# Attention with normalized queries and keys, then an MLP: a new order for batch 0, four score tiles in some bursts, and 64 by 64 tiles for three batches

## Chip, cores and metric

The kernel runs on one core of a Trainium2 chip, in one launch. The metric is the time of one execution on the device, in microseconds (us). Four executions of the kernel before gave 436.19 to 438.37, with a median of 438.2.

## What is computed

```python
B, H, S, D = 8, 12, 448, 64          # batches, heads, positions, head size
q_n, k_n = rmsnorm(q, g_q), rmsnorm(k, g_k)
attn = softmax(q_n @ k_n.T / 8)      # each batch and head by itself
x = (attn @ v) -> (B * S, H * D)     # heads side by side: 3584 x 768
h = x @ w_in                         # w_in 768 x 2048
g = max(h, 0) + alpha * min(h, 0)    # alpha per column of h, between 0 and 0.3
out = g @ w_out                      # w_out 2048 x 768, out 3584 x 768, float32
```

## The kernel before, in words

**Groups.** The 12 heads of a batch are handled in 3 groups of 4 heads (two pairs in each half of the partitions); groups are numbered through all batches, so batch b has groups 3b, 3b+1 and 3b+2, 24 in all. In a group's score tile (`score`, line 223) keys lie on the 128 partitions: 64 keys of two heads, with 448 queries for each of two columns ("par"). A group has 7 such tiles (j from 0 to 6). Each tile is exponentiated by ScalarE (`soft`, line 241, with a constant in place of the maximum) from PSUM into fp16. There are two PSUM buffers for score tiles.

**Tiles of the array.** Scores contract over 64 rows and so use half of the array's rows per matmul. Line 226 sets how many columns one matmul takes: 64 in batch 0 (4 matmuls to a tile), 32 in all other batches (8 matmuls to a tile). `over_keys` (line 249) sums over keys, with the exponentials as the moving operand: for the softmax's denominators (`den`, weights of ones) and for the values (`attv`). It works on a pair of groups (the first two of a batch, always 32 columns: 56 matmuls) or on the batch's third group by itself (line 251: 64 columns for group 2, 28 matmuls, else 32 columns, 56 matmuls). For a pair, `attv` runs twice, for even columns of the values (half 0) and for odd ones (half 1).

**PSUM.** There are three pools: two buffers of two banks for scores ("sc"), one buffer of two banks for denominators, values and turns ("acc"), and two single banks for the MLP ("mm"). Half 0 of the values goes to "acc" and half 1 to the two "mm" banks. A step may use "acc" in place of an "mm" bank when the plan calls it spare (`bank`, line 313; names hTa and opa in the profile).

**Preparing queries and keys.** For each group: load (SP's queue, `load_qk`), square (POOL), sum of squares (`reduce`, VectorE), `root` (ScalarE: a log and an exponential), scaling to fp16 (`scale`, mostly POOL), and a transposition. The first 6 groups are transposed by PE and copied out of PSUM by VectorE (`turn`, line 186; tiles tps in "mm", tps2 in "acc"). The others are transposed by DMA on SP's queue (`turn_dma`), and `turn` then only multiplies K by the gains on VectorE.

**MLP.** `up` (line 342) is one block of 128 columns of h: 6 matmuls, then ScalarE multiplies by alpha and VectorE takes the maximum into gT. `down` (line 355) is one 128 by 384 block of the output: 16 matmuls, a copy by VectorE, and two stores on SP's queue. For batch 0 the first four `up` blocks are begun before the last third of their input is there (`begin`, line 333) and finished later.

**The order of the work** is written out by the program before anything is issued; no scheduler reorders it. Lines 389 to 425 pack score tiles into numbered bursts of 2 or 3 tiles, and say in which burst the denominators (`dens`) and the values (`avs`) of a pair or a group fall. Lines 435 to 467 attach loads, squares, sums, roots and turns to bursts. Lines 470 to 539 share `up` and `down` steps out over the bursts, by estimated costs. The loop at line 589 then issues burst by burst: up to two score tiles, their exponentials, denominators or values, a third tile (and for pairs the second half of the values behind it), then the MLP steps of the burst. Within an engine, and within a DMA queue, instructions run in that order. Idle stretches of PE early on are filled with matmuls whose output is not used (`spin`). "First full unit" below is the first `up` that was not begun early: 6 matmuls at 46.16 us.

Of the kernel before, what the change touches and what calls it, by code (L numbers as in the profile page):

```python
# [21 lines left out]
def kernel(  # L22
# [17 lines left out]
    J = S // 64  # L40
    HH = H // 2
    G = HH // 2
# [5 lines left out]
    FB = DF // 4  # L48
    TD = min(6, NG)
    EB = 3  # L50
    assert G == 3

    cst = ctx.enter_context(tc.tile_pool(name="cst", bufs=1))
# [132 lines left out]
    def turn(y):  # L186

        if y >= TD:
            t = qkT[y, "k"].rearrange("p j g c -> p (j g c)")
            nc.vector.tensor_scalar(  # L190
                out=t, in0=t, scalar1=gain[:, 0:1], scalar2=None, op0=ALU.mult
            )
            return
        if y < G:
            ps = [psf.tile([128, 512], FP32, name="tps", tag="mm") for _ in "qk"]
        else:
            ps2 = psa.tile([128, 2, 512], FP32, name="tps2", tag="acc")
            ps = [ps2[:, 0], ps2[:, 1]]
        tps = [
            t[:, : S].bitcast(FP16).rearrange("p (j c) -> p j c", j=J) for t in ps  # L200
        ]
        for tp, nm in zip(tps, "qk"):
            for j in range(J):
                nc.tensor.transpose(  # L204
                    tp[:, j, :], qs[y, nm][:, j].rearrange("p h d -> p (h d)"), ident
                )
        for tp, nm in zip(tps, "qk"):
            t = att.tile([128, J, 2, 64], FP16, name=f"{nm}T", tag=f"{nm}T", bufs=4)
            o = t.rearrange("p j g c -> p j (g c)")
            if nm == "q" and y == 0:  # L210
                nc.scalar.copy(out=o, in_=tp)
            elif nm == "q":
                nc.vector.tensor_copy(out=o, in_=tp)
            else:
                nc.vector.tensor_scalar(  # L215
                    out=o, in0=tp, scalar1=gain[:, 0:1], scalar2=None, op0=ALU.mult
                )
            qkT[y, nm] = t
# [4 lines left out]
    def score(y, j):  # L223
        qT, kT = qkT[y, "q"], qkT[y, "k"]
        sc = pss.tile([128, 2, 512], FP32, name="sc", tag="sc")
        m = 64 if y < G else 32
        for c in range(64 // m):
            for par in range(2):
                for g in range(2):
                    nc.tensor.matmul(  # L230
                        out=sc[ds(64 * g + m * c, m), par, :S].rearrange(
                            "p (j c) -> p j c", j=J
                        ),
                        lhsT=kT[ds(64 * par, 64), j, g, ts(c, m)],
                        rhs=qT[ds(64 * par, 64), :, g, :],
                        start=True,
                        stop=True,
                    )
        scs[y, j] = sc

    def soft(y, j):
        if j == 0:
            expT[y] = att.tile([128, J, 2, S], FP16, name="expT", tag="expT", bufs=EB)
        nc.scalar.activation(  # L244
            out=expT[y][:, j], in_=scs[y, j][:, :, :S], func=AF.Exp,
            scale=QK_SCALE, bias=expb[:, 0:1],
        )

    def over_keys(accs, ys, weights):

        m = 64 if ys == (G - 1,) else 32
        if len(ys) == 2:
            heads = [(y, par, 0) for y in ys for par in range(2)]
        else:
            heads = [(ys[0], par, c) for par in range(2) for c in range(64 // m)]
        for j in range(J):
            for h, (y, par, c) in enumerate(heads):
                for g in range(2):
                    nc.tensor.matmul(  # L259
                        out=accs[g][ds(m * h, m), :S],  # L260
                        lhsT=weights(g, y, par, ts(c, m), j),
                        rhs=expT[y][ds(64 * g, 64), j, par, :],
                        start=(j == 0),
                        stop=(j == J - 1),
                    )
# [17 lines left out]
    def attv(ys, half, spare=False, jobs=()):  # L283

        b, i = divmod(ys[0], G)
        v2 = vt[b].rearrange("p h j (d e) -> p h j d e", e=2)

        def weights(g, y, par, c, j):
            h = 2 * (y - G * b) + par
            if len(ys) == 1:  # L290
                return vt[b][ds(64 * g, 64), h, j, c]
            return v2[ds(64 * g, 64), h, j, :, half]

        if half:
            av, accs = None, [psf.tile([128, 512], FP32, name="avb", tag="mm") for _ in range(2)]
        else:
            pool, tag = (pss, "sc") if spare else (psa, "acc")
            av = pool.tile([128, 2, 512], FP32, name="av", tag=tag)
            accs = (av[:, 0], av[:, 1])
        over_keys(accs, ys, weights)  # L300
        for f in jobs:
            f(ys)
        if b not in xT:
            xT[b] = att.tile([128, 2, G, S], FP16, name="xT", tag="xT")
        x, r = xT[b][:, :, i + half, :], rden[ys]
        if half:
            for g in range(2):
                nc.vector.tensor_mul(out=x[:, g], in0=accs[g][:, :S], in1=r[:, g])
        else:
            nc.vector.tensor_mul(out=x, in0=av[:, :, :S], in1=r)  # L310
# [22 lines left out]
    def begin(ft):  # L333

        if ft < 2:
            begun[ft] = bank("hT", False)
        elif ft == 2:
            t = psa.tile([128, 2, 512], FP32, name="hTb", tag="acc")
            begun[2], begun[3] = t[:, 0], t[:, 1]
        up_part(begun[ft], 0, ft, 0, G - 1)  # L340
# [55 lines left out]
    while m < NG * J or steps:  # L396
        n = len(bursts)
        while steps:
            ys, values = steps[0]
            if values:  # L400

                if n in dens and ys != (G - 1,):
                    break
                avs[n] = ys
                av_at.update((y, n) for y in ys)
            else:
                if n in avs or any(last_in.get(y, n) >= n for y in ys):
                    break
                dens[n] = ys
                den_at.update((y, n) for y in ys)  # L410
            steps.pop(0)
        late = len(avs.get(n, ())) == 2 or n in dens and n in avs or any(y >= G for y in dens.get(n, avs.get(n, ())))
        bursts.append([])
        while len(bursts[n]) < (3 if late else 2) and m < NG * J:
            y, j = divmod(m, J)
            if j == 0 and y >= EB and av_at.get(y - EB, n) == n:

                if y - EB not in av_at:
                    break
                split[n] = min(len(bursts[n]), 2)  # L420
            bursts[n].append((y, j))
            first_in.setdefault(y, n)
            if j == J - 1:
                last_in[y] = n
            m += 1
# [10 lines left out]
        y: max(n for n in range(first_in[y]) if y >= TD or n not in dens)  # L436
        for y in range(1, NG)
    }
    turn_at[2] = 5
    turn_at.update((y, den_at[y - 2]) for y in range(TD, NG) if y % G == 1)  # L440
    turns = {n: y for y, n in turn_at.items()}
    jobs = {}
    for y in range(G, NG):

        early = y < G + 2
        if early:
            n = turn_at[y - 1] + (y == G)
        elif y == G + 2:
            n = den_at[G - 1]
        elif y == 2 * G:  # L450
            n = turn_at[y] - 4
        elif y == 2 * G + 1:
            n = den_at[G] - 1
        elif y % G:
            n = den_at[y - 3 if y % G == 1 else y - G]
        else:
            n = av_at[y - 4]
        at(n - (6 if early else 4 if y <= 3 * G else 5), load_qk, y)
        for nm in "qk":
            (after if early else at)(n - 2, square, y, nm)  # L460
            if early:
                after(n, reduce, y, nm)
            else:
                jobs.setdefault(n, []).append((reduce, (y, nm)))
        roots[n + 1] = y
# [123 lines left out]
    for n in range(NB):  # L589
# [5 lines left out]
        first_tiles = tiles[: split.get(n, 2)] if not lead else tiles  # L595
        for t in first_tiles:
            score(*t)
            if lead and t == tiles[0]:
                soft(*t)
                den(dens[n])  # L600
                attv(avs[n], 0, True, (log, invert))
            elif lead and t == tiles[1]:
                begin(1)
                begin(2)
        plain = lead or n not in dens and n not in avs
        wait = plain and not lead and gaps[n] and gaps[n][0][0] is up
# [4 lines left out]
        if n in dens and not lead:  # L611
            den(dens[n])
        if n in avs and not lead:
            attv(avs[n], 0)
        for t in tiles[len(first_tiles) :]:
            score(*t)
            soft(*t)
        if n in avs and len(avs[n]) == 2:
            attv(avs[n], 1)
        late = []  # L620
        if wait:
            late = [(1, soft, t) for t in tiles[1:]]
# [50 lines left out]
                    late = []  # L673
        if not gaps[n] and n in turns:
            turn(turns[n])
        if n == den_at[G - 1] - 1:
            begin(0)
        for _, g, c in late:
            g(*c)
        if n < den_at[G - 1] - 1 and plain and n not in turns:  # L680
# [35 lines left out]
```

## Time and profile before

| what | value |
|---|---|
| median of four executions | 438.2 us |
| the profiled execution | 438.37 us, of which its span is 436.6 us |
| mean granted clock of TensorE | 0.994 |
| PE busy | 416.0 us, 5241 matmuls and as many weight loads |
| ScalarE (ACT) busy | 277.2 us |
| VectorE (DVE) busy | 208.9 us |
| POOL busy | 175.6 us |
| DMA | 53.88 MB, mean 123 GB/s over the span |
| 16 matmuls of `down`, between two others | 2.60 us |
| 6 matmuls of `up`, between two others | 1.14 us |
| one exponential of a score tile (ACT) | 1.00 us, 0.93 in a row |

How to read the profile: PE is TensorE's stream of matmuls, PEld its weight loads beside it. A row of the order of time gives the start, the length, the engine, the line of the kernel, the operation, output and inputs, the tile of the array (64*32: 64 rows by 32 columns), the shape, a count of equal instructions in a row, and in brackets the idle time before it with what ended it. The ends of matmuls are modelled, so lengths of runs are best taken from start to start. "issue" is a wait that ends on nothing the profile shows. In the waits by releaser the numbers are the total in us, how often, and the longest.

### The profile page before, as it was taken

Reading aid. Unit: us, or ns where it says so; the run is one execution under the profiler, and the core shown is the slowest. Engines: PE = TensorE matmul, PEld = TensorE weight load, DVE = VectorE, ACT = ScalarE, POOL = GpSimd, SP = SyncE. Lnnn points to the kernel's source line nnn. Section 1 sums busy time; section 2 is a strip of 40 time slices with the busy share of each in tenths; the row PEclk is TensorE's granted clock in tenths of the full one; section 3 lists DMA queues with packets and bytes.
Section 4 is the critical chain, followed back from the end, with each engine's and each line's share of the span. In section 5 each row is a group of like instructions: output and inputs, shape, how many; then the busy total and the mean of one; then the engine's idle time right before and its main releaser. Section 6 shows DMA issues by size and latency. Waiting matters only on the chain.

```text
span 436.6 us, 12032 instructions
## 1 busy us (share of the span) xinstructions
PE 416.0 (95%) x5241; PEld 215.2 (49%) x5241; DVE 208.9 (48%) x303; ACT 277.2 (63%) x385; POOL 175.6 (40%) x133
## 2 busy tenths in 40 slices
PE   7779999799999999999999999999999999999996
PEld 3334445354555445544555445444555445555563
DVE  3756664444574356535554356535553353233421
ACT  4897888368977576768847576758837577132300
POOL 5799878436273625283073625174043000000000
PEclk9999999989999999999999999999999999999999
DMA  8999999988449831997069841984064300211033
GB/s 191 238 231 199 207 236 187 198 178 179 95 82 185 194 96 25 168 186 179 21 113 177 183 101 26 174 163 110 20 101 102 77 1 21 57 37 36 20 73 73
DMA packets 70229, 53.88 MB, mean 123 GB/s; under 512 B 37392, under 2 KB 70176, under 8 KB 70176
## 3 DMA queue, kind: packets, MB, share of 16 engines
q1 hardware_dynamic: 55456, 40.19, 42.9%
q0 software_dynamic: 13984, 11.81, 18.4%
q10 hardware_dynamic: 736, 1.11, 1.0%
q8 instruction: 41, 0.67, 0.6%
q14 instruction: 12, 0.10, 0.1%
HBM read 45.62 MB, written 11.01 MB: 130 GB/s over the span
## 4 chain that ended last, share of the span: by engine, by line
PE 87%; ACT 6%; DVE 3%; issue 2%; DMA 1%; SPq 0%; ACTq 0%
PE op L359 29%; PE hT L325 20%; PE hTa L325 10%; PE sc L230 8%; PE opa L359 6%; PE dn L259 5%; PE av L259 5%; ACT expT L244 3%; PE avb L259 3%; DMA nat<-in_k_dram 1%; ACT ah L352 1%; DVE ss L152 1%; DVE gT L353 1%; PE tps L204 1%; DVE kT L215 0%
## 5 line engine op out<-in xcount | busy, mean ns | idle before, releaser
L244 ACT ACTIVATE expT<-sc,expb 128x896 f16<-128x896 f32 x168 | 160.4, 1003 | 41.4 <-PE sc L230 40.6
L359 PE MATMUL op<-w_out_sb,gT 128*128 128x384 f16 x752 | 131.2, 330 | 0.0
L169 POOL TENSOR_TENSOR qs<-nat,rr 128x896 f16<-128x896 f32 x44 | 76.7, 1761 | 111.9 <-ACT rr L164 82.4
L359 PEld LDWEIGHTS <-gT 128*128 128x128 f16 x896 | 85.0, 98 | 67.3 <-issue 14.7
L325 PEld LDWEIGHTS <-w_in_sb 128*128 128x128 f16 x768 | 73.2, 98 | 73.6 <-issue 9.2
L325 PE MATMUL hT<-xT,w_in_sb 128*128 128x448 f16 x516 | 108.1, 353 | 0.9 <-DVE gT L353 0.9
L146 POOL TENSOR_TENSOR sq<-nat 128x896 f32<-128x896 f32 x44 | 73.2, 1679 | 49.0 <-DMA nat<-in_q_dram 23.7
L352 ACT ACTIVATE ah<-hT,cols 128x448 f16<-128x448 f32 x86 | 54.3, 633 | 47.3 <-PE hT L325 47.3
L353 DVE TENSOR_TENSOR gT<-hT,ah 128x448 f16<-128x448 f32 x86 | 53.6, 624 | 56.5 <-ACT ah L352 56.4
L369 DVE COPY osb<-op 128x384 f32<-128x384 f32 x47 | 26.2, 557 | 80.1 <-PE op L359 77.5
L230 PE MATMUL sc<-qT,kT 64*32 64x448 f16 (+1 forms) x1260 | 53.3, 355 | 7.1 <-ACT expT L244 4.3
L152 DVE TENSOR_REDUCE ss<-sq 128x14 f32<-128x896 f32 x48 | 49.9, 1077 | 7.0 <-ACT sq L144 6.2
L325 PE MATMUL hTa<-xT,w_in_sb 128*128 128x448 f16 x240 | 51.9, 353 | 0.0
L352 ACT ACTIVATE ah<-hTa,cols 128x448 f16<-128x448 f32 x40 | 25.4, 634 | 31.4 <-PE hTa L325 31.4
L353 DVE TENSOR_TENSOR gT<-hTa,ah 128x448 f16<-128x448 f32 x40 | 25.0, 624 | 28.5 <-ACT ah L352 28.5
L230 PEld LDWEIGHTS <-kT 64*32 64x32 f16 (+1 forms) x1260 | 15.2, 90 | 37.9 <-issue 32.5
L310 DVE TENSOR_TENSOR xT<-av,rden 128x896 f16<-128x896 f32 x16 | 17.5, 1092 | 21.2 <-PE av L259 19.3
L259 PE MATMUL dn<-expT,ones 64*32 64x448 f16 (+1 forms) x868 | 24.5, 350 | 2.9 <-issue 2.1
L259 PEld LDWEIGHTS <-vt 64*32 64x32 f16 (+1 forms) x1316 | 19.5, 93 | 14.2 <-issue 2.9
L359 PE MATMUL opa<-w_out_sb,gT 128*128 128x384 f16 x144 | 24.9, 327 | 0.0
L259 PE MATMUL av<-expT,vt 64*32 64x448 f16 (+1 forms) x868 | 24.1, 349 | 0.7 <-ACT rden L276 0.7
L259 PEld LDWEIGHTS <-ones 64*32 64x32 f16 (+1 forms) x868 | 13.0, 93 | 11.7 <-issue 4.3
(43 smaller groups left out, 163.2 us busy)
## 6 DMA issues: line engine op xcount, KB each, us to landing
out_dram<-osb SPq DMA_DIRECT2D x110, 96.0 KB, 2.3
nat<-in_q_dram SPq DMA_DIRECT2D x46, 224.0 KB, 4.9
nat<-in_k_dram SPq DMA_DIRECT2D x46, 224.0 KB, 5.6
vt<-in_v_dram POOLq DMA_DIRECT2D x16, 336.0 KB, 6.8
w_in_sb<-in_moe_w_in_dram POOLq DMA_DIRECT2D x12, 256.0 KB, 7.5
w_out_sb<-in_moe_w_out_dram POOLq DMA_DIRECT2D x4, 768.0 KB, 15.4
nat<-in_q_dram ACTq DMA_DIRECT2D x2, 224.0 KB, 4.7
nat<-in_k_dram ACTq DMA_DIRECT2D x2, 224.0 KB, 6.0
```

The source lines that it names most:

```text
L146: nc.gpsimd.tensor_mul(out=sqf, in0=src, in1=src)
L152: nc.vector.tensor_reduce(out=ss_t[y][:, "qk".index(nm)].rearrange("p h j -> p (h j)").unsqueeze(2), in_=sqs[y, nm], axis=AXIS_X, op=ALU.add,)
L169: eng.tensor_mul(out=t.rearrange("p j h d -> p h j d"), in0=nat[y, nm], in1=rr_t[y][:, "qk".index(nm)].unsqueeze(3).broadcast_to((128, 2, ...
L230: nc.tensor.matmul(out=sc[ds(64 * g + m * c, m), par, :S].rearrange("p (j c) -> p j c", j=J), lhsT=kT[ds(64 * par, 64), j, g, ts(c, m)], r ...
L244: nc.scalar.activation(out=expT[y][:, j], in_=scs[y, j][:, :, :S], func=AF.Exp, scale=QK_SCALE, bias=expb[:, 0:1],)
L259: nc.tensor.matmul(out=accs[g][ds(m * h, m), :S], lhsT=weights(g, y, par, ts(c, m), j), rhs=expT[y][ds(64 * g, 64), j, par, :], start=(j = ...
L310: nc.vector.tensor_mul(out=x, in0=av[:, :, :S], in1=r)
L325: nc.tensor.matmul(out=hT[:, :S], lhsT=w_in_sb[:, g * G + i, ts(ft, 128)], rhs=xT[b][:, g, i, :], start=(i == 0 and g == 0), stop=(i == G ...
L352: nc.scalar.activation(out=ah, in_=hT[:, :S], func=AF.Copy, scale=alpha_sb[:, ft : ft + 1])
L353: nc.vector.tensor_max(out=gT[:, ft, ds((b & 1) * S, S)], in0=hT[:, :S], in1=ah)
L359: nc.tensor.matmul(out=op[:, :OH], lhsT=gT[:, ft, ts(t, 128)], rhs=w_out_sb[:, ft, ds(oh * OH, OH)], start=(ft == 0), stop=(ft == NF - 1),)
L369: nc.vector.tensor_copy(out=o, in_=op[:, :OH])
```

## The change

- A constant `EARLY = 3 * G` makes groups 0 to 8 (batches 0 to 2) use 64 columns per matmul for scores, and groups 2, 5 and 8 for denominators and values by themselves.
- A burst with the values of a pair from batch 1 on may hold four score tiles. The fourth comes after the second half of the values, and it may be the first tile of a group whose exponentials take over the buffer that these values free. Three bursts fewer are needed (69 in place of 72). Turns and preparations attached to bursts shift with that: the first group of a batch is scaled and transposed by DMA in the burst of the pair's denominators, no longer in that of its values.
- In batch 0, odd columns of the first pair's values come first, then even ones, then the third score tile and behind it the turn of group 3, which now uses the "mm" banks. The first two early `up` blocks come in the burst after that, ahead of its exponentials.
- Due times: preparations of group 6 are attached one burst earlier, so that its sums fall between `up` steps. In the order of the queues, group 6's squares come before group 5's scaling on POOL, and group 6's DMA transposes before group 8's loads on SP.

In the program's order, 280 matmuls and 280 weight loads fewer are issued. The core of the diff:

```diff
+    EARLY = 3 * G
...
-        if y < G:
+        if y <= G:
             ps = [psf.tile([128, 512], FP32, name="tps", tag="mm") for _ in "qk"]
...
-        m = 64 if y < G else 32
+        m = 64 if y < EARLY else 32
...
-        m = 64 if ys == (G - 1,) else 32
+        m = 64 if len(ys) == 1 and ys[0] < EARLY else 32
...
-        late = len(avs.get(n, ())) == 2 or n in dens and n in avs or any(y >= G for y in dens.get(n, avs.get(n, ())))
+        both = len(avs.get(n, ())) == 2
+        late = both or n in dens and n in avs or any(
+            y >= G for y in dens.get(n, avs.get(n, ()))
+        )
+        limit = 2 + late + (both and avs[n][0] >= G)
         bursts.append([])
-        while len(bursts[n]) < (3 if late else 2) and m < NG * J:
+        while len(bursts[n]) < limit and m < NG * J:
             y, j = divmod(m, J)
             if j == 0 and y >= EB and av_at.get(y - EB, n) == n:
 
-                if y - EB not in av_at:
+                if y - EB not in av_at or both and len(bursts[n]) < 3:
                     break
...
-    turn_at[2] = 5
+    turn_at[2], turn_at[G] = 5, av_at[0]
...
-            n = turn_at[y - 1] + (y == G)
+            n = turn_at[y - 1] + 1
...
-        elif y == 2 * G + 1:
-            n = den_at[G] - 1
+        elif y % G == 1:
+            n = den_at[y - 4] - 1
         elif y % G:
-            n = den_at[y - 3 if y % G == 1 else y - G]
+            n = den_at[y - G]
...
             score(*t)
-            if lead and t == tiles[0]:
+            if n == den_at[G - 1] - 1 and t == tiles[-1]:
+                begin(0)
+                begin(1)
+            elif lead and t == tiles[0]:
                 soft(*t)
                 den(dens[n])
                 attv(avs[n], 0, True, (log, invert))
             elif lead and t == tiles[1]:
-                begin(1)
                 begin(2)
...
-            attv(avs[n], 0)
-        for t in tiles[len(first_tiles) :]:
+
+            for half in (1, 0) if avs[n] == (0, 1) else (0,):
+                attv(avs[n], half)
+        for t in tiles[len(first_tiles) : 3]:
             score(*t)
             soft(*t)
-        if n in avs and len(avs[n]) == 2:
+        if n in avs and len(avs[n]) == 2 and avs[n] != (0, 1):
             attv(avs[n], 1)
+        for t in tiles[max(len(first_tiles), 3) :]:
+            score(*t)
+            soft(*t)
...
-        if n == den_at[G - 1] - 1:
-            begin(0)
```

## Prediction

> **What bounds the kernel now.** I read the chain of waits first, then PE's order of time, then PE's own waits, then the clock stage by stage. The chain says where a saving counts:
>
> ```profile
> PE 87%; ACT 6%; DVE 3%; issue 2%; DMA 1%; SPq 0%; ACTq 0%
> ```
>
> TensorE (PE) is 87% of the chain. From the first MLP unit at 46.16 us to PE's last matmul at 432.3 us it is hardly ever idle, so there a microsecond counts only if it is one of PE. Before 46 us the chain runs through ScalarE's exponentials and the first turns. A second item is small but concentrated: "issue", 2%. PE's waits by releaser, without any time of day:
>
> ```profile
> PE sc L230 <- ACT expT L244: 4.3, 10, 0.7
> PE dn L259 <- issue: 2.1, 1, 2.1
> PE avb L259 <- issue: 0.9, 1, 0.9
> PE sc L230 <- issue: 0.8, 1, 0.8
> PE dn L259 <- DVE osb L369: 0.6, 1, 0.6
> ```
>
> Three waits release on nothing the profile shows. PE's order of time places two of them (start, duration, tile, count, idle before):
>
> ```profile
> 76.44 0.57 PE L259 MATMUL avb<-expT,vt 64*32 64x448 f16 x12
> 77.88 1.32 PE L259 MATMUL avb<-expT,vt 64*32 64x448 f16 x44 [0.88 <-issue]
> 79.13 2.77 PE L359 MATMUL opa<-w_out_sb,gT 128*128 128x384 f16 x16
> 81.84 0.57 PE L230 MATMUL sc<-qT,kT 64*32 64x448 f16 x16
> 82.56 1.50 PE L259 MATMUL dn<-expT,ones 64*32 64x448 f16 x52
> 86.13 0.37 PE L259 MATMUL dn<-expT,ones 64*32 64x448 f16 x4 [2.08 <-issue]
> 86.15 0.55 PE L230 MATMUL sc<-qT,kT 64*32 64x448 f16 x8
> 86.62 4.45 PE L359 MATMUL op<-w_out_sb,gT 128*128 128x384 f16 x16
> ```
>
> Both stops fall in the middle of a run of equal matmuls, so no operand is missing. Between them lie 44+16+16+52 = 128 matmuls, each with its weight load: 256 instructions. The third stop (280.96 us) lies 5376 = 21x256 instructions further, PE's separate waits counted. And a queue of its own carries instructions:
>
> ```profile
> q8 instruction: 41, 0.67, 0.6%
> ```
>
> 0.67 MB in 41 packets is 16 KB each. I read: PE's program arrives in blocks of 256 instructions, a block is asked for when the one before it starts, and PE stops when that took longer than a block lasts (71.15 to 77.88 us: 6.7 us; 77.88 to 86.13: 8.3 us; 275.50 to 282.11: 6.6 us). The second stop costs more than itself (PE's busy time, then the other engines', clock, DMA share):
>
> ```profile
> 83.51:86.92 3.41, 1.33 (x34) 0.45 (x19) 0.98 (x1) 0.83 (x2) 3.10 (x4) 1.00 1.27 183
> 86.92:90.33 3.41, 3.41 (x13) 1.67 (x11) 0.45 (x1) 2.61 (x3) 0.08 (x1) 0.50 1.05 185
> ```
>
> After 3.4 us with PE 39% busy the clock is 0.50 for the next 3.4 us, and op needs 4.39 us start to start instead of 2.71.
>
> Price of the stops, start to start against the same run undisturbed: avb 2.69-1.43, dn 3.59-1.32, sc and op at half clock 0.18+1.68, sc at 281 1.44-0.30: **6.5 us**.
>
> **The change part by part.** The profiled execution took 438.37 us (span 436.6), 0.2 above the median; sums are against it.
>
> *64 by 64 tiles for groups 3 to 8.* A score tile is 4 matmuls instead of 8, a single group's den or values 28 instead of 56: 6x7x4 + 4x28 = 280 matmuls and 280 weight loads fewer. Streaming gains nothing: 28 matmuls of 64x64 take 1.35 us (38.29 to 39.64), 56 of 64x32 take 1.32. What it costs is switches. Pairs of groups keep 64x32, so scores and pairs now differ. The Trainium skill ("TensorEngine Tiling (Array Packing)", Key Properties) says that changing the tiling mode drains the array, which speaks against this. The rows: 64x64 score (28.04) to 64x32 dn (28.35) is 0.31 for 0.19 of streaming, so 0.12 a switch; 128 to 64x32 and back are 0.09 and 0.13. If a drain exposed a whole matmul (0.35 against 0.19) a switch would be 0.16 and 15 of them 2.4 us; by the row 1.9. I take the row. Counted in the program's order from the first full MLP unit on: 15 switches 64/32 appear in batches 1 and 2.
>
> *Four tiles in values' bursts, three bursts fewer.* Score and MLP work are unchanged, but 128/small switches fall from 122 to 116: -6x0.11 = -0.7. Switches together **+1.2**.
> A values' burst now ends in one down on the spare (den's) banks, and the next burst needs those after two score tiles: the row 81.84 to 82.56 shows that wait, 0.34 more than two tiles take. Before, this came after group 4 and the last values' burst; now also after 7, 10, 13, 16 and 19, where a second unit used to lie between: 0.22 + 4x0.34 = **+1.6**. The fourth score tile itself needs its banks' exponential, done about 1 us earlier (exponentials 0.93 each); VectorE's multiply of an earlier turned K (0.45 to 1.4) has MLP work beside it. Both nothing.
>
> *Batch 0.* Values of odd columns go to MLP banks, so they need not wait for the log that frees den's banks (0.73 of idle ahead of 31.10); even columns follow; the turn of group 3 and two early units fill PE while VectorE copies. Before, den of group 2 started at 38.29 behind the turned K (37.25+0.68). After: exponentials run from 31.94 without a gap, five to 36.6; PE could be there at 37.0. A block boundary falls on the third values matmul; its refill took 5.0 us before (31.11 to 36.11). Asked for near 30.0 it comes at 35.0, 0.6 after PE wants the next scores (34.4). So den at 37.35: **-0.9** (between -1.3 without that stop and -0.3 if the refill is no earlier). From den to the first full unit the chain (log, invert, multiply, scores, exponential, unit) is as before, 7.9 us.
>
> *Moved steps.* Group 6's squares now stand before group 5's scaling on POOL (2x1.66 us): group 5 is needed four bursts later. Its reductions come a burst earlier, between units 9 to 11: VectorE then has 3x0.62+2x1.08 for 3.4 us of PE, gT of unit 11 ends about 0.8 late for unit 13, whose bank it frees: **+0.8** (0 to 0.9). In later batches the spare banks fall so that nothing waits. ScalarE's root of group 6 (0.55) is a burst earlier too: scores' waits on exponentials between 50 and 67 us (0.72, 0.39, 0.39, 0.67, start to start) change places, not their sum. Group 6's two DMA transposes pass group 8's loads on SP: those wait until about 69 us (51.85 before), its squares hold POOL's scaling of group 7, whose turned K was copied at 87.18. I get 86 to 89 after; scores need it at about 91: nothing, but with 2 us of cover.
>
> *Instruction stops.* The skill ("Runtime: NRT & Kernel Launch", Instruction fetch mechanics) says that crossing a block boundary is mostly hidden. By that, 560 fewer instructions are worth nothing and the sum is +2.7. The rows show 6.5. I laid the blocks over the new order: those that start near 68, 75 and 82 us last 7.4, 6.5 and 13.8 us; before, those of 61.94, 71.15 and 77.88 lasted 9.2, 5.5 and 6.0, less their stops. Against 6.6 to 8.3 us of refill: one stop of about 1 at den of group 5 and no halved clock. Left: **1.1** (0 to 6.5 and more), so -5.4.
>
> Sum: -0.9+1.2+1.6+0.8-5.4 = -2.7: 435.7 on the profiled execution, 435.5 on the median.
>
> **The rivals.**
> - *All goes* (0.13): no stop, head -1.3, unit 13 not late: -1.3+1.2+1.6-6.5 = -5.0, 433.2. For it: w_out, which fills the DMA queues until 75 us, ends sooner without group 8's loads beside it.
> - *Clock halves again* (0.20): loads of groups 8 and 9 now follow each other and the refill of 75 us waits behind them as at 77.88: a stop of 2.3 and 1.7 of half clock instead of 1.1: +2.9, 438.4.
> - *Group 8 late* (0.06): its loads land only when group 9's did (82), scaling and transposes follow, scores wait some 2.5 us: 438.0.
> - *Slower* (0.11): the transposes of groups 9, 12, 15, 18, 21 move from the values' burst into the den burst before it, and land in PE's densest stretch: in the next burst of batch 3 a block lasts 3.0 us (128 matmuls of 64x32), in batches 4 to 6 5.4 to 5.9. With refills of 6.6 us, as at 275.50, which began 2 to 4 us after such transposes (271.39, 273.19): 3.6+1.7 of half clock and some 0.6 in the others: +6, 441.4. It decides from 6 us of stops in all. Against it: the refill at 187.1, half a microsecond after transposes (186.54), lost nothing.
>
> **How the numbers follow.** Likeliest (0.50): 435.5, its own range 434.3 to 436.8. A measurement of this kernel tells 0.5% from no change, 2.2 us: 436.0 and 440.4. Faster: all goes, and four fifths of the likeliest: 0.53. Slower: 0.10. Same: 0.37. The range 432.8 to 439.6 takes in all but the slower case and some edges.
>
> **What would show it.** Right: PE's "issue" waits total under 1.5 us; clock 1.00 at 80 to 95 us; first full unit near 45.3; waits of den on VectorE's copy six or seven times; scores and den 64x32 at 0.12 switches. Wrong: a clock of 0.50 after 50 us; "issue" waits in the values' bursts of batches 3 to 6; waits of scores on turned K near 91 us.

## The result and the profile after

The changed kernel takes 436.22 us (median of 32 executions, 434.74 to 439.35). The kernel before, run in turn with it on the same chip, takes 438.63 (53 executions, 434.9 to 441.43). The ratio is 0.9954, with a 95% interval of 0.9939 to 0.9969. Executions of over 1.5% above the fastest of their kernel are left out of all ratios and of the counts of clocks below. By the ratio the gain is 0.46%, or 2.0 us, just inside the 0.5% that was named as the bound of "no change"; its interval reaches to both sides of that bound, and the two medians lie 2.4 us (0.55%) apart. The forecast of 435.5 lies 0.7 us below the median.

The profiled execution of the changed kernel took 438.12 us (span 436.3). So it shows one of the longer executions, and its profile has to be read with that in mind. The chain by engine:

```profile
PE 84%; ACT 4%; DMA 4%; DVE 4%; POOL 2%; issue 1%; SPq 0%; ACTq 0%
```

DMA (1% before) and VectorE (DVE, 3% before) have grown in the chain. PE's waits by releaser show where:

```profile
PE sc L231 <- ACT expT L245: 3.5, 8, 0.7
PE avb L260 <- DVE osb L370: 2.1, 1, 2.1
...
PE sc L231 <- issue: 1.2, 1, 1.2
...
PE dn L260 <- DVE osb L370: 0.6, 1, 0.6
```

The three "issue" waits of before (2.1, 0.9 and 0.8) are down to one of 1.2. In their place stands a wait of 2.1 of the odd values (avb) on VectorE's copy of an output block. PE's order of time puts it where the first stop was:

```profile
76.56 0.38 PE L231 MATMUL sc<-qT,kT 64*64 64x448 f16 x4
76.87 0.36 PE L260 MATMUL avb<-expT,vt 64*32 64x448 f16 x1
79.32 2.75 PE L260 MATMUL avb<-expT,vt 64*32 64x448 f16 x55 [2.08 <-DVE osb L370]
82.00 0.59 PE L231 MATMUL sc<-qT,kT 64*64 64x448 f16 x4
82.52 2.92 PE L360 MATMUL opa<-w_out_sb,gT 128*128 128x384 f16 x16
85.37 0.57 PE L231 MATMUL sc<-qT,kT 64*64 64x448 f16 x8
86.09 1.52 PE L260 MATMUL dn<-expT,ones 64*64 64x448 f16 x28
87.41 0.39 PE L231 MATMUL sc<-qT,kT 64*64 64x448 f16 x4
```

The denominators (dn) of group 5 now run as 28 matmuls without a break. The odd values start with one matmul into the first MLP bank and then wait for the second bank. VectorE's order of time says what the copy of that bank (osb) waited for:

```profile
69.75 0.56 DVE L370 COPY osb<-op 128x384 f32<-128x384 f32 x1
78.34 0.45 DVE L191 TENSOR_SCALAR kT<-kT,gain 128x896 f16<-128x896 f16 x1 [8.04 <-DMA kT<-qs]
78.71 0.55 DVE L370 COPY osb<-op 128x384 f32<-128x384 f32 x1
```

Ahead of the copy stands the multiply of group 6's transposed K, and it waits until 78.34 for the DMA transpose, which SP issued at 66.31. The multiply itself takes 0.45 us. The pause also cost clock (PE busy, then the other engines', granted clock, DMA share, GB/s):

```profile
76.70:80.10 3.40, 1.31 (x29) 0.62 (x33) 1.76 (x3) 1.30 (x2) 0.00 (x0) 0.90 1.07 179
80.10:83.50 3.40, 3.40 (x57) 1.40 (x41) 1.31 (x3) 0.86 (x1) 2.27 (x2) 0.60 1.08 217
83.50:86.90 3.40, 3.25 (x40) 1.85 (x42) 1.43 (x2) 1.24 (x3) 3.40 (x3) 1.00 0.96 205
```

From 79.43 to 82.84 us the clock is 0.50, after a stretch in which PE was about 39% busy, as before. It is why 55 matmuls of avb take 2.75 us here and 56 take 1.5 elsewhere. In batch 0 there is a second find. These are rows of the kernel before, then of the changed one:

```profile
37.98 0.38 PE L230 MATMUL sc<-qT,kT 64*32 64x448 f16 x8 [0.55 <-DVE kT L215]
38.29 1.52 PE L259 MATMUL dn<-expT,ones 64*64 64x448 f16 x28
...
46.16 1.29 PE L325 MATMUL hT<-xT,w_in_sb 128*128 128x448 f16 x6 [0.40 <-DVE gT L353]
```

```profile
33.44 0.96 PE L205 MATMUL tps<-ident,qs 128*128 128x128 f16 x14
34.32 0.37 PE L231 MATMUL sc<-qT,kT 64*64 64x448 f16 x1
35.90 0.57 PE L231 MATMUL sc<-qT,kT 64*64 64x448 f16 x7 [1.20 <-issue]
36.40 1.69 PE L326 MATMUL hT<-xT,w_in_sb 128*128 128x448 f16 x8
38.02 0.38 PE L231 MATMUL sc<-qT,kT 64*64 64x448 f16 x4
38.23 0.55 PE L260 MATMUL dn<-expT,ones 64*64 64x448 f16 x8
```

A stop in the middle of eight equal score matmuls takes what the new order had won. The denominators of group 2 start at 38.23, against 38.29 before, and the first full unit at 45.98, against 46.16.

**Clock over all executions.** Every timed execution also has a mean granted clock. Half clock for 3.4 of some 434 us lowers that mean by 3.4 x 0.5/434 = 0.004, so an execution at 0.998 or more can't hold such a stretch. In the changed kernel 22 of 33 executions are at 0.998 or more, with a median of 436.03 us; the other 11 have a median of 437.98. Of the kernel before, 202 executions taken beside the experiments give 33 at 0.998 or more, with a median of 435.74, and 169 below, with 438.84. Where the clock stays up the two kernels take about the same time. What differs is how often it stays up: 16% of executions before (11% to 28% in the four series of experiments), 67% after. The two shares were not measured in turn, since the clocks of the 53 executions beside the changed kernel are not on record. The mean also doesn't say where the clock fell: in the profiles of experiments 2, 3 and 4 a stretch of half clock lies in the first 18 us. The profile of after shows one of the remaining third.

### The profile page after: what moved, and what is told of

It reads as the page before. It is cut to its first block, busy times and chain, and to the rows that moved or that the text cites. A ratio compares the mean times of both kernels' runs of the same rounds, so it can differ in the third digit from the quotient of the medians.

```text
span 436.3 us, 11474 instructions
## 1 busy us (share of the span) xinstructions
PE 416.8 (96%) x4961; PEld 215.3 (49%) x4961; DVE 203.8 (47%) x303; ACT 278.7 (64%) x385; POOL 174.7 (40%) x133
## 4 chain that ended last, share of the span: by engine, by line
PE 84%; ACT 4%; DMA 4%; DVE 4%; POOL 2%; issue 1%; SPq 0%; ACTq 0%
PE op L360 27%; PE hT L326 20%; PE hTa L326 10%; PE sc L231 7%; PE opa L360 6%; PE dn L260 5%; PE av L260 4%; PE avb L260 3%; DMA kT<-qs 3%; ACT expT L245 3%; DMA nat<-in_k_dram 1%; DVE osb L370 1%; PE tps L205 1%; DVE ss L153 1%; POOL sq L147 1%
## 5 line engine op out<-in xcount | busy, mean ns | idle before, releaser
L360 PE MATMUL op<-w_out_sb,gT 128*128 128x384 f16 x736 | 126.1, 327 | 0.0
L326 PE MATMUL hT<-xT,w_in_sb 128*128 128x448 f16 x510 | 106.9, 353 | 0.8 <-DVE gT L354 0.8
L353 ACT ACTIVATE ah<-hT,cols 128x448 f16<-128x448 f32 x85 | 53.7, 633 | 46.8 <-PE hT L326 46.8
L326 PE MATMUL hTa<-xT,w_in_sb 128*128 128x448 f16 x246 | 53.2, 353 | 0.0
L360 PE MATMUL opa<-w_out_sb,gT 128*128 128x384 f16 x160 | 27.9, 328 | 0.0
```

Of the source, the lines that this page charges most:

```text
L326: nc.tensor.matmul(out=hT[:, :S], lhsT=w_in_sb[:, g * G + i, ts(ft, 128)], rhs=xT[b][:, g, i, :], start=(i == 0 and g == 0), stop=(i == G ...
L353: nc.scalar.activation(out=ah, in_=hT[:, :S], func=AF.Copy, scale=alpha_sb[:, ft : ft + 1])
L360: nc.tensor.matmul(out=op[:, :OH], lhsT=gT[:, ft, ts(t, 128)], rhs=w_out_sb[:, ft, ds(oh * OH, OH)], start=(ft == 0), stop=(ft == NF - 1),)
```

## The experiments

Twelve kernels were run, each timed in turn with the kernel before (the ratios below are to it, with their 95% intervals). The question for all: which part gives the gain, and where did the rest of the predicted gain go?

**1. The parts alone.** First, the kernel before with nothing but the wider tiles:

```diff
+    EARLY = 3 * G
-        m = 64 if y < G else 32
+        m = 64 if y < EARLY else 32
-        m = 64 if ys == (G - 1,) else 32
+        m = 64 if len(ys) == 1 and ys[0] < EARLY else 32
```

> The kernel before with one part of the change alone: 64 by 64 tiles for scores of groups 3 to 8 and for den and values of groups 5 and 8. My theory (PE stops for blocks of instructions; fewer instructions take the stops away): 15 switches and their like cost 1.9 us of PE, and the stops at 77, 84 to 91 us (5.4 us with the halved clock) shrink to 0 to 1.5: 2 to 3.5 us faster than before, that is about 435.5 to 436.5, with PE's issue waits between 70 and 95 us under 1.5 us. Rival 1 (the stops belong to the DMA traffic of that moment and not to the number of instructions): they stay, and the switches are paid: 1.5 to 2 us slower than before. Rival 2 (the gain of the whole change comes from batch 0 and the fewer bursts): again 1.5 to 2 slower.

Measured: 435.86 us, ratio 0.9933 (0.9908 to 0.9959). Then the changed kernel without the wider tiles:

```diff
-    EARLY = 3 * G
+    EARLY = G
```

> The changed kernel with 64 by 32 tiles again from group 3 on; everything else of the change stays. My theory: 1.9 us of switches are saved, and two stops come back near 76 and 83 us (1.2 and 2.7 us, and a halved clock with 1.7): 2 to 4 us slower than the changed kernel, 438 to 440. Rival 1 (stops by DMA traffic, which the change moved by putting group 6's transposes ahead of group 8's loads): no stops, 1.5 to 2 us faster than the changed kernel, about 434.5. Rival 2 (gain from batch 0 and fewer bursts): likewise faster by the switches.

Measured: 437.51 us, ratio 0.9998 (0.9975 to 1.0021). Its waits by releaser:

```profile
PE avb L260 <- issue: 1.6, 1, 1.6
PE sc L231 <- issue: 1.1, 1, 1.1
PE dn L260 <- DVE osb L370: 0.6, 1, 0.6
```

The stop in avb is back, and the one at the scores of batch 0 is there too. So the wider tiles alone give all of the gain, and the rest of the change without them is worth nothing that can be measured. The wider tiles alone don't remove every stop either. PE's order of time in that kernel:

```profile
80.41 0.57 PE L231 MATMUL sc<-qT,kT 64*64 64x448 f16 x8
81.13 0.95 PE L260 MATMUL dn<-expT,ones 64*64 64x448 f16 x16
84.64 0.76 PE L260 MATMUL dn<-expT,ones 64*64 64x448 f16 x12 [2.56 <-issue]
```

Its clock stays at 1.00 behind this stop; 10 of its 20 executions have a mean clock of 0.998 or more, against 10 of 69 of the kernel before, run in turn with it. The end of a window of the clock lay inside this stop (see the last section), so that it cost no clock was luck in this execution.

**2. Is it the end of an instruction block?** If a stop falls where 256 instructions end, then instructions put in far ahead of it must move it. In both kernels, half of the 22 idle matmuls at the start gave way to 75 tiny ones, 128 instructions more in all, whose output is not used:

```diff
-    spin(22)
+    spin(11)
+    ps = psf.tile([128, 512], FP32, name="tiny", tag="mm")
+    for _ in range(75):
+        nc.tensor.matmul(out=ps[:, :16], lhsT=ident, rhs=idle[:, :16], start=True, stop=True)
```

> The kernel before, whose first 22 idle matmuls are replaced by 11 of them and 75 of 16 columns: 64 matmuls and weight loads, 128 instructions, more ahead of everything, and no other edit. If PE stops where a block of 256 instructions ends, every stop moves to 128 instructions earlier in the work: the first into the even values of groups 3 and 4 or none there (0.3 us), the second to the score tiles after the down in the values' burst (about 2 us), a third may come in the values of group 5 (1.2), and that of 281 us moves or goes; none stays at the 13th odd-values matmul or at the 53rd den matmul. Total within 1.5 us of before. If an operand or a buffer stops PE, the stops stay at the same matmuls.

Measured: 437.65 us, ratio 0.9990 (0.9962 to 1.0018). PE's order of time in the shifted kernel before:

```profile
81.65 0.37 PE L230 MATMUL sc<-qT,kT 64*32 64x448 f16 x4
85.86 0.93 PE L230 MATMUL sc<-qT,kT 64*32 64x448 f16 x12 [3.84 <-issue]
86.22 3.19 PE L259 MATMUL dn<-expT,ones 64*32 64x448 f16 x56
```

The stop was in dn, behind 52 of its 56 matmuls. It is now 64 matmuls (128 instructions) earlier: 52 of dn and 12 of the two score tiles. The stop belongs to a place in the instruction stream and not to an operand. It also grew to 3.8 us, and from 84.61 us on the clock is at half for 6.83 us.

> The changed kernel with the same 128 instructions more at the head. In it PE stopped at the second score tile matmul of the burst after batch 0's values (34.3 us, 1.6 us start to start), at a block's end. My theory: with the block's end 128 instructions earlier, between odd and even values, that block has 5 us and the stop goes: den of group 2 starts 0.9 to 1.5 us earlier than 38.23, and the first full unit at 44.6 to 45.2 in place of 45.98, the total 0.8 to 1.5 faster than the changed kernel. Rival: the scores there wait for something else (exponentials, the copied K): the first full unit stays within 0.3 us, the total too.

Measured for the shifted changed kernel: 437.39 us, ratio 0.9990 (0.9968 to 1.0011). The gain expected in batch 0 missed: the stop left the scores but moved into the even values, and one of 1.57 came into avb at 80.6. PE's order of time in batch 0:

```profile
34.54 1.32 PE L260 MATMUL av<-expT,vt 64*32 64x448 f16 x45 [1.88 <-issue]
35.79 0.38 PE L231 MATMUL sc<-qT,kT 64*64 64x448 f16 x4
36.11 0.96 PE L205 MATMUL tps<-ident,qs 128*128 128x128 f16 x14
```

From here to the old place, behind the first matmul of the next scores, there are 45+4+14+1 matmuls: 64 again. A block's end can be shifted; as long as the refill is slow it stops PE wherever short matmuls stand.

**3. Why are the refills slow?** The kernel before, without the loads of w_out for the second half of the output's columns (1.5 MB). POOL writes zeros there at the start, so all matmuls are issued, and the second half of the output is zero:

```diff
+    nc.gpsimd.memset(w_out_sb[:, :, OH:], 0.0)
-    for c in range(4):
+    for c in range(2):
```

> The kernel before without the loads of w_out's second half of columns (1.5 MB, set to zero at the start instead, so the output's second half of columns is zero); all matmuls stay. If the refill of an instruction block is slow because the DMA queues are full then, the stops of 77 and 84 us fall from 3.5 us to under 1 and the clock does not halve: 3.5 to 5.5 us faster than before, about 434. Rival (a refill takes 7 to 8 us whatever else runs, the instructions alone decide): both stops stay within 0.5 us, and the time within 1 us.

Measured: 433.13 us (4 executions), ratio 0.9875 (0.9828 to 0.9923). Same matmuls, same blocks, and PE's order of time has no gap where 0.9 and 2.1 were lost:

```profile
76.86 1.52 PE L259 MATMUL avb<-expT,vt 64*32 64x448 f16 x56
78.31 2.77 PE L359 MATMUL opa<-w_out_sb,gT 128*128 128x384 f16 x16
81.01 0.57 PE L230 MATMUL sc<-qT,kT 64*32 64x448 f16 x16
81.73 1.52 PE L259 MATMUL dn<-expT,ones 64*32 64x448 f16 x56
83.05 0.38 PE L230 MATMUL sc<-qT,kT 64*32 64x448 f16 x8
```

The DMA share from 60 to 75 us is 1.05 here and 1.28 before. So the stops hang on other transfers that the refills compete with. By the ratio this kernel takes 1.25% or 5.5 us less than the one before, about what the prediction had priced the stops and their half clock at (6.5).

**4. The wait for group 6's K.** If the place of the multiply on VectorE makes the wait, a later place removes it. In the next kernel it comes one burst later, behind the values. (The first score tile of group 6 is then taken without the gains.)

```diff
-            jobs.setdefault(n, []).append((turn, (turns[n],)))
+            jobs.setdefault(n + (turns[n] == 2 * G), []).append((turn, (turns[n],)))
```

> The changed kernel, but VectorE multiplies the turned K of group 6 one burst later, in the down of the values' burst, as before the change. In the changed kernel's trace VectorE stood 8.0 us on the DMA of this K with the copy of a finished down behind it, and PE waited 2.1 us for that copy's bank at the odd values (76.9 us), and ran 3.4 us at half clock after. My theory: that wait goes, 1 to 3 us faster than the changed kernel, 433.5 to 435.3. Rival: PE then meets the end of a block of instructions there (its block starts at 75.7 and its refill needs 6 to 8 us), or scores of group 6 wait for the same K: 0 to 0.7 us faster.

Measured: 436.21 us, ratio 0.9958 (0.9938 to 0.9977). The wait at avb is gone, and in the profile two stops stand for it: 2.43 at the scores of batch 0 (half clock from 37.66 to 41.07) and 1.54 in dn of group 5. The rival, which expected a stop at the next block's end instead, held. The next kernel adds to this one that a `down` of the pair's denominator burst moves into its values' burst in batches 3 to 6, which should end four of the waits of 0.34 there:

```diff
+    for n in range(first, NB - 1):
+        if n in dens and len(avs.get(n + 1, ())) == 2 and len(gaps[n]) == 2 and len(gaps[n + 1]) == 1:
+            gaps[n + 1].insert(0, gaps[n].pop())
```

> The changed kernel with group 6's K multiplied a burst later, and in batches 3 to 6 one down moved from the pair's den burst to its values' burst, so that a second unit lies between the spare down and the next den. Worked out: four waits of 0.34 us for VectorE's copy go (1.4), and the wait on group 6's K (1 to 3): 2 to 4 us faster than the changed kernel, 432 to 434. Rival: the exponentials no longer have that down beside them and scores wait instead: the 1.4 does not come, and only the first part is seen.

Measured: 435.06 us, ratio 0.9945 (0.9923 to 0.9967); the expected 432 to 434 was missed. From start to start, the four waits of 0.34 are gone, as they should be. A stop of 1.97 in dn of group 5 with half clock behind it (85.64 to 89.05) and one of 1.54 in batch 0 are in the profile.

**5. The fourth score tile.** The changed kernel with three tiles per burst at most, so 72 bursts again, and batch 0's order and the due times as changed:

```diff
-        limit = 2 + late + (both and avs[n][0] >= G)
+        limit = 2 + late
-                if y - EB not in av_at or both and len(bursts[n]) < 3:
+                if y - EB not in av_at:
```

> The changed kernel without the fourth score tile: 72 bursts again, in batches 3 to 6 a second unit again between a spare down and the next den; group 6 is again scaled and turned a burst later. Worked out: den's waits on VectorE's copy fall from seven to two or three (1.6 us), switches rise by 6 (0.6 us), the wait on group 6's K goes (up to 3): 1 to 3 us faster than the changed kernel, about that of the 64 by 64 tiles alone. Rival (fewer bursts are a gain): 0.5 to 1.5 slower than the changed kernel.

Measured: 439.86 us, ratio 1.0025 (0.9998 to 1.0051); expected was a gain over the changed kernel. K of group 6 is no longer waited for (its first scores come a burst later). But `up` waits twice for gT (1.17 each at 205 and 305 us, start to start, where the kernel before had 0.39), and batch 0 has its stop (1.78) with half clock behind. So packing four tiles does not cost more than it gives; the rest costs more when it stands without it. Set beside experiment 1, which differs only in batch 0's order and the due times, this kernel takes 4 us more (by the ratios, 0.9%). Batch 0 explains about 2.9 of it in the profiles (first full unit at 48.27 against 45.38) and the two gT waits 1.6. Against the changed kernel, which has the same order in batch 0, it loses 0.7% or 3 us; of these only the 1.6 of the two waits are explained, and the rest stays open.

**6. Batch 0's order.** The changed kernel with the order of before in batch 0 (even columns first, group 3's turn late and in its old bank, the early units where they were); tiles, fourth tile and due times stay:

```diff
-        if y <= G:
+        if y < G:
-    turn_at[2], turn_at[G] = 5, av_at[0]
+    turn_at[2] = 5
-            n = turn_at[y - 1] + 1
+            n = turn_at[y - 1] + (y == G)
-            for half in (1, 0) if avs[n] == (0, 1) else (0,):
+            for half in (0,):
...
```

> The changed kernel with batch 0's order of the kernel before: batch 0's values even columns first, group 3 turned late, the MLP's first units started where they were. 64 by 64 tiles, fourth tiles and new due times stay. Theory (the new order packs instruction blocks so densely at 28 to 36 us that one ends at scores whose refill isn't there, and this takes back its own gain): no stop over 0.5 us at the scores after batch 0's values, first full unit 45.4 to 46.2 us, time 0.5 to 2 us under the changed kernel, ratio to the kernel before 0.990 to 0.995. Rival (batch 0's new order is worth the 0.9 us it was predicted, and what is missing is lost later): first full unit 46 to 47 us and time 1 us over the changed kernel, ratio 0.997 to 0.999. In both the wait for K of group 6 at the odd values near 79 us stays (1.5 to 2.5 us).

Measured: 436.33 us, ratio 0.9958 (0.9937 to 0.9979). Its profile has no stop at batch 0's scores, and the first full unit is at 45.78. By the median it takes what the changed kernel takes, so neither theory's time held. The wait for K of group 6, expected at 1.5 to 2.5 us, was 0.68. The profiles of all kernels, sorted by batch 0's order, say more of that stage:

| batch 0's order | first full unit, us |
|---|---|
| before | 46.16, 45.38, 47.10 (shifted), 46.56, 45.78, 45.38, 46.11, 45.52 |
| changed | 45.98, 46.42, 47.19 (shifted), 48.90, 48.27, 46.48 |

Each number is one execution. With the changed order, every one of the six has a stop on "issue" that ends between 34.5 and 37.3 us, of 1.09 to 2.43; with the old order none has one of over 0.3 there. The medians are 45.9 and 46.8: the order loses rather than wins, in the profiles.

**7. All known losses at once.** The kernel of experiment 6, the multiply of group 6's K behind the copy of the first MLP bank but ahead of its first scores, and the moved `down`:

```diff
+            late_k = turns[n] == 2 * G
-            jobs.setdefault(n, []).append((turn, (turns[n],)))
+            (post if late_k else jobs).setdefault(n, []).append((turn, (turns[n],)))
```

> The run with batch 0's old order, and two moves: VectorE multiplies K of group 6 after it has copied out the first MLP bank of the values' burst (still ahead of the first scores of group 6), and one down accumulation goes from the pair's sum burst to its values' burst in batches 3 to 6. Theory (PE loses at waits that can be moved one by one, as long as no block's end falls into a burst of short instructions): no wait for VectorE's copy at the odd values near 79 us, the four waits of 0.34 us in batches 3 to 6 gone (1.4 us), time 432.5 to 435, ratio 0.986 to 0.992. Rival (what is taken away at one place comes back as a stop at the next block's end, as in the runs that moved only K of group 6): one or two issue stops of 1.5 to 3 us between 75 and 92 us and half clock after one, ratio 0.993 to 0.997.

Measured: 435.75 us, ratio 0.9936 (0.9914 to 0.9958): inside the rival's band. But the cause isn't the rival's: among PE's waits by releaser none is on "issue". PE's order of time:

```profile
76.27 1.52 PE L260 MATMUL avb<-expT,vt 64*32 64x448 f16 x56
79.01 0.38 PE L231 MATMUL sc<-qT,kT 64*64 64x448 f16 x4 [1.22 <-DVE kT L191]
80.00 4.44 PE L360 MATMUL opa<-w_out_sb,gT 128*128 128x384 f16 x16 [0.61 <-DVE xT L311]
84.37 0.57 PE L231 MATMUL sc<-qT,kT 64*64 64x448 f16 x8
```

The odd values run through, and now the fourth score tile, the first of group 6, waits for that K itself. VectorE takes it up at 78.50, when the transpose lands. The wait has changed its place by 2 us, and half clock (80.32 to 83.73) follows again. So another place for the multiply in VectorE's queue is not enough: the fourth tile needs K of group 6 at about 78 us, and it isn't there.

**8. Which groups need the wider tiles?** The kernel of experiment 1 and the one of experiment 7 with 64 by 64 tiles for groups 3 to 5 only:

```diff
-    EARLY = 3 * G
+    EARLY = 2 * G
```

> The kernel before with 64 by 64 tiles for groups 3 to 5 only (batch 1); groups 6 to 8 stay at 32 columns. Theory (64 by 64 tiles gain because groups 3 to 5 halve their instructions where the refills of PE's instruction blocks are slow, up to 91 us; later the refills keep up and the wider tiles only cost mode switches and longer chains): no stop over 1.5 us after 91 us, 0.75 us less matmul time than with groups 3 to 8, time 0.3 to 1 us under that run, ratio 0.990 to 0.993. Rival (groups 6 to 8 need the wider tiles too, because their bursts of scores and values from 92 to 145 us are as dense): issue stops of 1 to 3 us or half clock between 92 and 145 us, ratio 0.995 to 0.999.

Measured: 436.59 us, ratio 0.9940 (0.9914 to 0.9966).

> The run with batch 0's old order, the later multiply of K of group 6 and the moved down, with 64 by 64 tiles for groups 3 to 5 only. Theory: 0.75 us less matmul time than with groups 3 to 8 and no stop over 1 us after 92 us, ratio 0.991 to 0.993. Rival: stops of 1 to 3 us or half clock between 92 and 145 us, where the bursts of four score tiles lie, ratio 0.995 to 0.999. In both the stretch 75 to 92 us is unchanged up to how the block ends fall there, which this edit does not move.

Measured: 436.56 us, ratio 0.9967 (0.9943 to 0.9991). No "issue" stop of over 0.2 us falls between 92 and 145 us in either profile, so batch 2's denominators and values do not need the wider tiles. But no time was won. The score tiles of group 6 are computed from 79 us on, still in the bad stretch. With 16 matmuls instead of 8 to two tiles, the stop in dn of group 5 lasts 3.0 us in the first kernel, with half clock for 6.83 us from 84.67 on, and 2.5 us in the second. The first kernel's ratio is within neither band, the second's lies in the rival's, but without the stops that the rival named. The cut would have to be made by time, not by batch.

None of these kernels that does all of the work beats the changed one beyond the intervals. The wider tiles alone (0.9933, with a few lines of edit) are as fast as the whole change (0.9954).

## Why the prediction was right, and where its sum was wrong

The median agrees with the forecast: 436.2 against 435.5. The gain of 0.46% lies just below the bound of "faster", which had the larger chance. But in the profiled execution the sum of -2.7 stands against -0.25 measured, so its terms have to be looked at. That the medians agree so closely is partly luck: batch 0 gave less than forecast and the wait for group 6's K was not forecast at all, while 1.35 us came from waits whose change the sum had left out or put at nothing. By its terms, start to start:

| term | predicted | profiled execution |
|---|---|---|
| batch 0 | -0.9 | -0.18 |
| switches and matmul time | +1.2 | +1.23 |
| denominators wait for VectorE's copy | +1.6 | +1.58 |
| unit 13 late behind group 6's sums | +0.8 | +0.57 |
| instruction stops and their half clock | -5.4 | -6.04 |
| odd values wait for group 6's K, with half clock | 0 | +4.05 |
| exponentials waited for, 50 to 67 us | 0 | -0.57 |
| two waits for gT (205 and 305 us) that are gone | not named | -0.78 |
| small, and the end | | -0.1 |

- **Switches, copies, unit 13** came as worked out. The row of the waits at 176.83 us, two score tiles and then dn 0.73 after their start, comes once in each of batches 1 to 6, 0.34 above its undisturbed length in batches 3 to 6:

```profile
176.83 0.57 PE L231 MATMUL sc<-qT,kT 64*32 64x448 f16 x16
177.56 0.76 PE L260 MATMUL dn<-expT,ones 64*32 64x448 f16 x24
```

For the array's tiling mode, the row's 0.12 a switch was the right choice; the dearer bound (0.16 for each of the 15 new ones) would have given +1.7 for that term where 1.23 was found.
- **Instruction stops.** The boundaries were placed rightly, and the rule that crossing one is mostly hidden would have given no gain here; experiments 2 and 3 show that it isn't hidden in this stretch. The remaining stop of about 1 us, forecast at dn of group 5, is not in the profiled execution; related kernels have it there (1.0 to 2.6 us in experiments 1, 4 and 5). The late stop at 281 us shrank to 0.34+0.17 at 325.
- **The step that failed** is the sentence on the fourth score tile: VectorE's multiply of an earlier turned K "has MLP work beside it. Both nothing." It counted the multiply's 0.45 us and not what the multiply waits for. With the fourth tile, K of group 6 is multiplied ahead of the copy that frees the second MLP bank, and its transpose was issued at 66.31 and landed at 78.3. Before, the transpose was issued at 68.8 and landed 10.8 us later, and the same multiply came after the values and met it already there:

```profile
80.31 0.45 DVE L190 TENSOR_SCALAR kT<-kT,gain 128x896 f16<-128x896 f16 x1
```

The prediction followed group 6's transposes only as something that delays group 8's loads. Issued 2.5 us earlier, K thus came only 1.3 us earlier, and the values' burst asked for it 3.4 us earlier than the multiply of before. Where it lands varies: PE's wait was 0.68 us in experiment 6 and 0.20 in the second kernel of experiment 1, against 2.08 here, where half clock followed as well.
- **Signs that had been named.** The "issue" waits total 1.2 us, under the 1.5 named as right, and the waits on VectorE's copy came. The half clock after 50 us is the sign that had been named as wrong, and it is there in this execution.
- **Batch 0.** The boundary falls on the third values matmul, as forecast. But that starts at 30.4 and not near 30.0, and the refill took 5.5 us and not the 5.0 of before: the scores went on at 35.90 and not at 35.0. All else (7.75 us from there to the first full unit, predicted 7.9) held. The mechanism was named, its size taken from one execution, and it scatters: 1.1 to 2.4 us of idle at that place in five kernels, and 1.9 a little earlier in the sixth. The profiles give it a loss of 0.9 us at the median, the times of experiment 6 neither loss nor gain; which is right stays open.
- **"Clock halves again"**, given 0.20 and 438.4, is what the profiled execution shows (438.12), though by another trigger: a wait for K and not a refill. Over all executions it is one third. **"Slower"** did not occur: in the bursts of batches 3 to 6 the profile of after has no stop of over 0.4 us. Where a `down` was moved between bursts, one of 0.88 and one of 1.29 came up near 331 us (the second kernels of experiments 4 and 8). **"Group 8 late"**: its loads were issued at 69.41, as expected at "about 69", but K of group 7 came at 91.14, 2 us beyond the upper end given, and the scores were not held up.

## What to carry to other kernels

When a step is moved earlier, ask first when its own input lands and who stands behind it in its engine's queue; its duration can be the smaller part of its cost (here 0.45 us against a wait of 2.08). Where a program loses time at ends of instruction blocks, fewer instructions in the stretch where the DMA queues are full is the edit that worked here. Moving single waits there mostly moved the loss. Before a profile is explained, look whether the profiled execution is one of the many or one of the few: here two thirds of the executions had a mean clock that excludes the half clock its profile shows.

## What the runs showed of the hardware

- Refills of PE's instruction blocks depend on what else the DMA queues carry: with 1.5 MB less of weights, PE had no stop on "issue" of 0.2 us or more, and the kernel took 5.5 us less (experiment 3).
- Half clock has a threshold of its own. Its starts lie a multiple of 3.413 us apart within a trace (in the profile of after 79.43 and 434.42, behind the last matmuls: 354.99 = 104 x 3.413; before 86.92 and 435.08: 102 x 3.413). So each trace can be cut into windows of 3.41 us. For the stops between 30 and 100 us that fell at full clock, PE's idle time inside one window decided: 1.78 (experiment 5), 1.80 (two waits, experiment 1), 1.83 (two waits, experiment 7), 1.97, 2.08 and more were followed by half clock; 1.54 and 1.57 were not. Three others straddle an end of a window, and the clock stayed up: 1.20 in the profile of after; 1.88 in the shifted changed kernel, with at most 1.3 on one side; and 2.56 in the wider tiles alone, where the end lies at 83.48 (estimated from that trace's half clock at 435.05), with 1.40 on one side and 1.16 on the other. For such stops the limit thus lies between 1.57 and 1.78, near half a window.
- Idle time is not the whole rule. A window already at half clock was followed by another one with less idle time: 1.26 in experiment 2, 0.79 in experiment 8 (84.67 to 88.08 us). And at the end of the kernel of experiment 7, behind its last 128 by 128 matmuls, a window with 1.86 us idle (428.48 to 431.89) was followed by full clock. Why is open. The windows of experiment 2 (the shifted kernel before):

```profile
84.60:88.00 3.40, 2.14 (x48) 1.00 (x56) 0.00 (x0) 1.53 (x2) 2.39 (x3) 0.50 1.26 214
88.00:91.40 3.40, 3.40 (x42) 1.34 (x27) 0.55 (x1) 1.95 (x3) 1.23 (x2) 0.50 0.81 113
```

- The Trainium skill ("TensorE: Matmul & The Clock Gate", What's actually happening) has such a free-running window of 3.413 us, and the traces agree; its advice to avoid idle gaps of over about 3 us ("Why this matters for your kernels") is too generous here, since 1.8 us in one window was enough.
- The same kernel, executed again, scatters by 5 to 7 us (434.9 to 441.4 for the kernel before, 434.7 to 439.4 for the changed one). The median of executions with and without a lowered clock differs by 3.1 us in the kernel before and by 2.0 in the changed one.
